# A bf16 feed-forward layer on one core: the first 512 tokens by three DMA transposes instead of five

## The chip, the cores and the metric

The kernel runs on one NeuronCore of a Trainium2 chip. The metric is the device time of one execution in microseconds (us). Six executions of the kernel before took 126.07 to 126.8 us, with a median of 126.53 us. One more execution was recorded by the hardware profiler; its views are what this document reads. A core has five engines that run side by side, each with its own instruction queue: TensorE (PE, matmuls), VectorE (DVE), ScalarE (ACT), GpSimd (POOL) and SyncE (SP, which here issues nearly all DMAs). Sixteen DMA engines move the data.

## The reference

```python
B, S, D, F = 1, 2048, 640, 1728        # x: [B,S,D], w1: [D,F], w2: [F,D], all bf16
h = jnp.einsum("bsd,df->bsf", x, w1)
h = silu(h)
out = jnp.einsum("bsf,fd->bsd", h, w2)
```

## The kernel before

TensorE contracts over the 128 partitions of its two operands. The contraction of the first matmul runs over D = 640, which is five tiles of 128 (`DT` is 5; the code counts them by `k` or `dt`). Both operands must therefore have D on the partitions. w1 has that already. x does not, so it is transposed on its way in: `turned` (L119) issues a DMA transpose on SP's queue which reads 512 tokens by 128 columns of x from DRAM and writes 128 partitions by 512 tokens of `xT` in SBUF. The 2048 tokens are four chunks of 512 (`SCH`), so x takes 4 x 5 = 20 such transposes.

The hidden dimension F = 1728 is 13 tiles of 128 and a tail of 64. The first layer writes hidden units on the partitions: for a chunk and a hidden tile `ft`, five matmuls of 128x128 by 128x512 add up in one PSUM bank, and ACT applies silu and writes `hT`. The second layer then contracts over `hT` with `w2s`; its results leave through `o_sb`. The second layer is not touched by the change.

The first chunk is done differently from the others, because its data has not all come yet. The loop over `k` is outside: `k_pass(k)` (L183) runs hidden tiles 0 to 7, one bank each, with contraction tile `k` alone. All eight banks are thus filled in five passes of eight matmuls. Pass `k` needs transpose `k` of the first chunk and slab `k` of w1 (rows `k` x 128 and on, the first 1024 columns, 256 KB). It waits for both (L193), which is the only thing that TensorE waits for in this stretch. The first slab comes in two halves, so that four matmuls of pass 0 need half a slab only. After the five passes, hidden tiles 8 to 12 of the first chunk follow, from two further loads of w1 (`FG`, tiles 8 to 10 and the rest). Then come chunks 1 to 3 with `k` inside, each after a wait for its transposes, and then the tail and the second layer.

The order of the issues is written out by hand, and a queue issues in that order:

- ACT issues the first half of slab 0 at the very start.
- SP issues transpose 0, the second half of slab 0, transpose 1, slab 1, transpose 2, slab 2, transpose 3, slab 3, transpose 4, slab 4, then the two `FG` loads, the 15 transposes of chunks 1 to 3, and the loads of w2.

What `ahead_of_start` wraps is moved in front of the start barrier of the program. On SP this holds for everything up to slab 1; the drain of the barrier stands behind it (L354 in the profile is where the program is built), and the rest follows. `barrier_wait_here` moves an engine's wait for the others to a later place: behind the `FG` loads on SP, behind pass 0 on PE.

`dummies(15)` (L172) are matmuls on a tile of zeros that nobody reads. They keep TensorE at work until the first data is there. They write bank 3, which pass 0 then overwrites.

Of the kernel before, what the change touches and what calls it, by code (L numbers as in the profile page):

```python
# [9 lines left out]
def bass_standalone__dense_activation_silu__prompt_kernel(  # L10
# [9 lines left out]
    xf = x.flatten_outer_dims()  # L20
# [3 lines left out]
    P = 128  # L24
    NB = 8
    BANK = 512
    DT = D // P
    FT = F // P
    FL = F - FT * P
    SCH = 512  # L30
# [7 lines left out]
    pe, act, dve, pool, sp = nc.tensor, nc.scalar, nc.vector, nc.gpsimd, nc.sync  # L38

    with ExitStack() as es:  # L40
        def sb(name, shape, dtype):
            return es.enter_context(nc.sbuf_tensor(name, shape, dtype))

        xT = sb("xT", [P, DT, S], bf16)
        w1s = sb("w1s", [P, DT, F], bf16)
# [13 lines left out]
        def sem(name):  # L59
            s = es.enter_context(nc.semaphore(name))  # L60
            count[s.name if hasattr(s, "name") else name] = 0
            return [s, 0]

        def tick(ins, s, n=1):
            ins.then_inc(s[0], n)
            s[1] += n
            return (s, s[1])

        def wait(eng, *points):
            for pt in points:  # L70
                if pt is None:
                    continue
                s, v = pt
                key = (id(eng), id(s))
                if seen.get(key, 0) < v:
                    eng.wait_ge(s[0], v)
                    seen[key] = v
# [6 lines left out]
        def load(eng, out_ap, in_ap):  # L84
            s = sem(f"s_ld{n_dma[0]}")
            n_dma[0] += 1
            return tick(eng.dma_start(out=out_ap, in_=in_ap), s, 16)  # L87

        ET = mybir.EngineType

        def preamble(engine, opcode):
            lst = nc.main_func.blocks[0].instructions
            return next(
                i for i, ins in enumerate(lst)
                if ins.opcode == opcode and ins.engine == engine
            )

        def ahead_of_start(emit, engine):
            lst = nc.main_func.blocks[0].instructions
            n = len(lst)  # L100
            r = emit()
            lst = nc.main_func.blocks[0].instructions
            new = lst[n:]
            del lst[n:]
            at = preamble(engine, "Drain")
            lst[at:at] = new
            return r
# [5 lines left out]
        w1_v = w1.rearrange("(dt p) f -> p dt f", p=P)  # L113
        w2_v = w2[0:F0, :].rearrange("(ft p) d -> p ft d", p=P)

        FA = 8
        FG = [(8, 11), (11, FT)]

        def turned(c, dt, s):  # L119
            return tick(sp.dma_start_transpose(  # L120
                out=xT[:, dt, c * SCH:(c + 1) * SCH],
                in_=xf[c * SCH:(c + 1) * SCH, dt * P:(dt + 1) * P],
            ), s, 16)

        def load_k(eng, k):
            return load(eng, w1s[:, k, 0:FA * P], w1_v[:, k, 0:FA * P])

        ld_w1 = {}
        s_x = [sem(f"s_x{k}") for k in range(DT)]
        p_z = ahead_of_start(lambda: tick(dve.memset(z[:, :], 0.0), s_dve), ET.DVE)  # L130
        ld_x = [ahead_of_start(lambda: turned(0, 0, s_x[0]), ET.SP)]
        FH = FA // 2
        ld_k0a = ahead_of_start(
            lambda: load(act, w1s[:, 0, 0:FH * P], w1_v[:, 0, 0:FH * P]), ET.Activation)
        ld_k = [ahead_of_start(
            lambda: load(sp, w1s[:, 0, FH * P:FA * P], w1_v[:, 0, FH * P:FA * P]), ET.SP)]
        ld_x.append(ahead_of_start(lambda: turned(0, 1, s_x[1]), ET.SP))
        ld_k.append(ahead_of_start(lambda: load_k(sp, 1), ET.SP))
        for k in range(2, DT):
            ld_x.append(turned(0, k, s_x[k]))  # L140
            ld_k.append(load_k(sp, k))
        for a, b in FG:
            e = F if b == FT else b * P
            pt = load(sp, w1s[:, :, a * P:e], w1_v[:, :, a * P:e])
# [8 lines left out]
        ld_xc = {}  # L153
        for c in range(1, NSC):
            s = sem(f"s_xc{c}")
            for dt in range(DT):
                ld_xc[c] = turned(c, dt, s)
        ld_w2 = [
            load(sp, w2s[:, 0:7, :], w2_v[:, 0:7, :]),
            load(sp, w2s[:, 7:FT, :], w2_v[:, 7:FT, :]),  # L160
# [6 lines left out]
        def dummies(n):  # L167
            for _ in range(n):
                pe.matmul(ps[:, 3, 0:HB], lhsT=z[:, 0:P], rhs=z[:, :], start=True, stop=True)  # L169

        wait(pe, p_z)
        dummies(15)  # L172

        def mm(o, l, r, start, stop, shared=False):
            return pe.matmul(o, lhsT=l, rhs=r, start=start, stop=stop, skip_group_check=shared)  # L175
# [7 lines left out]
        def k_pass(k):  # L183
            for ft in range(FA):
                if k == 0 and ft == FH:
                    wait(pe, ld_k[0])
# [35 lines left out]
        for q in range(NSC // 2):  # L222
            b = bank()
            for k in range(DT):
                for hh in range(2):
                    c = 2 * q + hh
# [92 lines left out]
        for q in range(NSC // 2):  # L319
            tt = []  # L320
            for hh in range(2):
                c = 2 * q + hh
# [3 lines left out]
            for hh in range(2):  # L326
                c = 2 * q + hh
# [3 lines left out]
                    out=o_sb[:, c * JB:(c + 1) * JB, DA:D],  # L331
                    in_=oT[:, c * SCH:(c + 1) * SCH],
# [36 lines left out]
```

## Time and profile before

| | |
|---|---|
| median of six runs | 126.53 us (126.07 to 126.8) |
| the profiled execution's own time | 126.29 us |
| its span, first to last instruction | 125.0 us |
| PE busy | 121.8 us, 97% of the span |
| ACT busy / DVE busy | 38.1 us / 7.5 us |
| DMA transposes of x | 20, issued at L120 on SP |
| matmuls in the dummies (L169) | 15, 3.38 us |
| first matmul of pass 0 / pass 1 / last pass | 3.57 / 6.44 / 12.42 us after the span's start |

A page of the profile has one line per group of instructions with the line of the code, the engine, the operation and the tiles it writes and reads. A "q" behind an engine (SPq) stands for its queue issuing a DMA, with the time that the issue holds the queue; that time is not the time of the transfer. The view by DMA gives the time from an issue's start to the landing of its data. "Idle before" is what an engine stood still, with the event that ended it. The chain that ended last follows the execution back from its last instruction, at each step to what released it.

### The profile page before, as it was taken

The page shows a single profiled execution, that of the slowest core. Times are in us where ns is not written, and L with a number is a line of the kernel's source. Part 1 is how long each engine was busy: PE and PEld are TensorE (multiplying, and loading weights), DVE is VectorE, ACT ScalarE, POOL GpSimd, SP SyncE. Part 2 cuts the span into 40 slices and gives each one's busy share as a digit, 9 for nine tenths or more (in the row PEclk, how much of TensorE's full clock was granted, in tenths as well). Part 3 has the DMA queues.
Part 4 walks back from the last instruction along what each step waited for, and adds up shares of the span by engine and source line. Part 5 has one row for each costly group of instructions (what it writes and reads, how often), then busy time and mean ns, then how long its engine had stood idle before and what let it go on. Part 6 is the DMA issues. An engine that isn't in the chain of part 4 may idle for free.

```text
span 125.0 us, 1354 instructions
## 1 busy us (share of the span) xinstructions
PE 121.8 (97%) x589; PEld 55.3 (44%) x589; DVE 7.5 (6%) x12; ACT 38.1 (30%) x66; POOL 0.3 (0%) x5
## 2 busy tenths in 40 slices
PE   8998999999999999999999999999999999999993
PEld 6342444444444444444434444444434443444452
DVE  0000000000000000000002020200012210112021
ACT  0400885555555555555530101010012011010100
POOL 0000000000000000000000000000000000000000
DMA  5789957454895000000000000000002868111112
GB/s 109 183 214 229 285 121 77 91 110 93 172 394 210 0 5 0 3 0 0 0 0 0 5 0 0 0 0 0 0 0 64 67 213 302 52 52 52 52 59 99
DMA packets 19541, 10.35 MB, mean 83 GB/s; under 512 B 13520, under 2 KB 19024, under 8 KB 19536
## 3 DMA queue, kind: packets, MB, share of 16 engines
q1 hardware_dynamic: 19392, 10.15, 32.2%
q10 hardware_dynamic: 144, 0.13, 0.4%
q8 instruction: 4, 0.07, 0.2%
q14 instruction: 1, 0.01, 0.0%
HBM read 4.51 MB, written 2.62 MB: 57 GB/s over the span
## 4 chain that ended last, share of the span: by engine, by line
PE 89%; SPq 7%; DMA 3%; issue 1%; ACT 0%
PE ps L175 89%; SPq L120 5%; DMA w1s<-in_w_dram 3%; SPq L87 2%; ACT o_sb L241 0%; SPq L354 0%
## 5 line engine op out<-in xcount | busy, mean ns | idle before, releaser
L175 PE MATMUL ps<-xT,w1s 128*128 128x512 bf16 (+1 forms) x280 | 59.6, 382 | 0.9 <-DMA w1s<-in_w_dram 0.7
L175 PE MATMUL ps<-w2s,hT 128*128 128x512 bf16 (+2 forms) x221 | 45.4, 367 | 0.0
L175 PEld LDWEIGHTS ps<-xT,w1s 128*128 128x128 bf16 (+1 forms) x280 | 26.4, 99 | 33.9 <-issue 3.4
L179 ACT ACTIVATE hT<-ps 128x512 bf16<-128x512 f32 x52 | 30.0, 608 | 26.8 <-PE ps L175 26.8
L175 PEld LDWEIGHTS ps<-w2s,hT 128*128 128x128 bf16 x221 | 20.9, 98 | 24.4 <-issue 1.1
L241 ACT CAST o_sb<-ps 128x512 bf16<-128x512 f32 (+1 forms) x8 | 4.4, 545 | 42.2 <-PE ps L175 42.2
L239 DVE CAST o_sb<-ps 128x512 bf16<-128x512 f32 (+1 forms) x9 | 6.1, 677 | 101.5 <-PE ps L175 101.5
L175 PE MATMUL ps<-hT,w2s 128*128 128x512 bf16 x52 | 11.4, 379 | 0.0
L175 PEld LDWEIGHTS ps<-hT,w2s 128*128 128x128 bf16 x52 | 5.1, 97 | 6.2
L241 ACT CAST oT<-ps 128x512 bf16<-128x512 f32 x2 | 1.1, 588 | 11.0 <-PE ps L175 11.0
L169 PE MATMUL ps<-z 128*128 128x256 bf16 x15 | 3.4, 416 | 0.4 <-DVE z L130 0.4
L169 PEld LDWEIGHTS ps<-z 128*128 128x128 bf16 x15 | 2.0, 142 | 1.2 <-DVE z L130 0.4
L151 ACT ACT_TABLE_LOAD x1 | 1.3, 1283 | 4.1 <-DVEq L354 4.1
L175 PE MATMUL ps<-w2t,hTt 64*128 64x512 bf16 (+2 forms) x17 | 2.2, 366 | 0.0
L239 DVE CAST oT<-ps 128x512 bf16<-128x512 f32 x2 | 1.3, 687 | 13.7 <-PE ps L175 13.7
L179 ACT ACTIVATE hTt<-ps 128x512 bf16<-128x512 f32 x2 | 1.2, 597 | 1.1 <-PE ps L175 1.1
L175 PEld LDWEIGHTS ps<-w2t,hTt 64*128 64x128 bf16 x17 | 0.7, 94 | 1.4 <-issue 0.8
L175 PE MATMUL ps<-hTt,w2t 64*128 64x512 bf16 x4 | 0.6, 381 | 0.0
L175 PEld LDWEIGHTS ps<-hTt,w2t 64*128 64x128 bf16 x4 | 0.1, 94 | 0.4 <-issue 0.4
L151 ACT ACTIVATE warm<-warm 128x32 f32<-128x32 f32 x1 | 0.2, 229 | 0.0
L130 DVE MEMSET z<- 128x128 uint32 x1 | 0.2, 165 | 0.2 <-issue 0.2
L149 POOL MEMSET warm<- 128x32 f32 x1 | 0.1, 124 | 3.7 <-POOLq L354 3.7
(4 smaller groups left out, 0.4 us busy)
## 6 DMA issues: line engine op xcount, KB each, us to landing
out_dram<-o_sb SPq DMA_DIRECT2D x15, 160.0 KB, 1.9
w2s<-in_w_dram SPq DMA_DIRECT2D x1, 1120.0 KB, 5.6
w1s<-in_w_dram SPq DMA_DIRECT2D x4, 256.0 KB, 3.2
w2s<-in_w_dram SPq DMA_DIRECT2D x1, 960.0 KB, 7.6
w1s<-in_w_dram SPq DMA_DIRECT2D x1, 480.0 KB, 4.3
w1s<-in_w_dram SPq DMA_DIRECT2D x1, 400.0 KB, 5.3
xT<-in_x_dram SPq DMA_TRANSPOSE x20, 3.6
w2t<-in_w_dram SPq DMA_DIRECT2D x2, 80.0 KB, 7.0
```

What stands on the lines that cost most here:

```text
L87: return tick(eng.dma_start(out=out_ap, in_=in_ap), s, 16)
L120: return tick(sp.dma_start_transpose(out=xT[:, dt, c * SCH:(c + 1) * SCH], in_=xf[c * SCH:(c + 1) * SCH, dt * P:(dt + 1) * P],), s, 16)
L130: p_z = ahead_of_start(lambda: tick(dve.memset(z[:, :], 0.0), s_dve), ET.DVE)
L149: p_warm = tick(pool.memset(warm[:, :], 0.0), s_pool)
L151: act.activation(out=warm[:, :], in_=warm[:, :], func=ACT.Silu)
L169: pe.matmul(ps[:, 3, 0:HB], lhsT=z[:, 0:P], rhs=z[:, :], start=True, stop=True)
L175: return pe.matmul(o, lhsT=l, rhs=r, start=start, stop=stop, skip_group_check=shared)
L179: r = tick(act.activation(out=out_ap, in_=in_ap, func=ACT.Silu), s_act)
L239: r = tick(dve.tensor_copy(out=out_ap, in_=in_ap), s_dve)
L241: r = tick(act.copy(out=out_ap, in_=in_ap), s_act)
```

## The change

The first chunk's five transposes become three. Their column ranges are `KT` = (0,1), (1,3), (3,5) in contraction tiles: one transpose of 512 x 128 and two of 512 x 256. A wide one writes two rows of `xT`'s middle dimension, and each of its two passes waits for the same semaphore. The same three pieces are used in chunks 1 to 3, so x takes 12 transposes instead of 20. SP's order becomes: transpose 0, second half of slab 0, slab 1, transpose of tiles 1 and 2 (all this ahead of the start barrier), slab 2, transpose of tiles 3 and 4, slab 3, slab 4, and then as before. The dummies go from 15 to 13.

```diff
-        def turned(c, dt, s):
+        def turned(c, k0, k1, s):
             return tick(sp.dma_start_transpose(
-                out=xT[:, dt, c * SCH:(c + 1) * SCH],
-                in_=xf[c * SCH:(c + 1) * SCH, dt * P:(dt + 1) * P],
+                out=xT[:, k0:k1, c * SCH:(c + 1) * SCH],
+                in_=xf[c * SCH:(c + 1) * SCH, k0 * P:k1 * P],
             ), s, 16)
...
-        s_x = [sem(f"s_x{k}") for k in range(DT)]
+        KT = [(0, 1), (1, 3), (3, DT)]
+        s_x = [sem(f"s_x{k0}") for k0, _ in KT]
+        ld_x = {}
+
+        def first(i):
+            k0, k1 = KT[i]
+            pt = turned(0, k0, k1, s_x[i])
+            for k in range(k0, k1):
+                ld_x[k] = pt
...
-        ld_x = [ahead_of_start(lambda: turned(0, 0, s_x[0]), ET.SP)]
...
+        ahead_of_start(lambda: first(0), ET.SP)
...
-        ld_k = [ahead_of_start(
-            lambda: load(sp, w1s[:, 0, FH * P:FA * P], w1_v[:, 0, FH * P:FA * P]), ET.SP)]
-        ld_x.append(ahead_of_start(lambda: turned(0, 1, s_x[1]), ET.SP))
-        ld_k.append(ahead_of_start(lambda: load_k(sp, 1), ET.SP))
-        for k in range(2, DT):
-            ld_x.append(turned(0, k, s_x[k]))
-            ld_k.append(load_k(sp, k))
+        ld_k[0] = ahead_of_start(
+            lambda: load(sp, w1s[:, 0, FH * P:FA * P], w1_v[:, 0, FH * P:FA * P]), ET.SP)
+        ahead_of_start(lambda: slab(1), ET.SP)
+        ahead_of_start(lambda: first(1), ET.SP)
+        slab(2)
+        first(2)
+        slab(3)
+        slab(4)
...
-            for dt in range(DT):
-                ld_xc[c] = turned(c, dt, s)
+            for k0, k1 in KT:
+                ld_xc[c] = turned(c, k0, k1, s)
...
-        dummies(15)
+        dummies(13)
```

More of the change, by code (lines that the diff above doesn't have):

```diff
@@ L128, in bass_standalone__dense_activation_silu__prompt_kernel, with slab @@
         ld_w1 = {}
-        s_x = [sem(f"s_x{k}") for k in range(DT)]
+        KT = [(0, 1), (1, 3), (3, DT)]
[6 more added lines that the diff above has]
+                ld_x[k] = pt
         p_z = ahead_of_start(lambda: tick(dve.memset(z[:, :], 0.0), s_dve), ET.DVE)
-        ld_x = [ahead_of_start(lambda: turned(0, 0, s_x[0]), ET.SP)]
         FH = FA // 2
+        ld_k = {}
+        def slab(k):
+            ld_k[k] = load_k(sp, k)
+        ahead_of_start(lambda: first(0), ET.SP)
         ld_k0a = ahead_of_start(
             lambda: load(act, w1s[:, 0, 0:FH * P], w1_v[:, 0, 0:FH * P]), ET.Activation)
-        ld_k = [ahead_of_start(
-            lambda: load(sp, w1s[:, 0, FH * P:FA * P], w1_v[:, 0, FH * P:FA * P]), ET.SP)]
-        ld_x.append(ahead_of_start(lambda: turned(0, 1, s_x[1]), ET.SP))
-        ld_k.append(ahead_of_start(lambda: load_k(sp, 1), ET.SP))
-        for k in range(2, DT):
-            ld_x.append(turned(0, k, s_x[k]))
-            ld_k.append(load_k(sp, k))
+        ld_k[0] = ahead_of_start(
[6 more added lines that the diff above has]
+        slab(4)
         for a, b in FG:
```

## The prediction

> **What bounds the kernel now.** I read the page first. TensorE is busy for 97% of the span, and the only thing in its group that it waits for is a w1 load (last columns: idle before, and what ended most of it).
>
> ```profile
> PE 121.8 (97%) x589; PEld 55.3 (44%) x589; DVE 7.5 (6%) x12; ACT 38.1 (30%) x66; POOL 0.3 (0%) x5
> ...
> L175 PE MATMUL ps<-xT,w1s 128*128 128x512 bf16 (+1 forms) x280 | 59.6, 382 | 0.9 <-DMA w1s<-in_w_dram 0.7
> ```
>
> The chain that ended last, in order of time, says where the rest is: up to 12.28 us it runs on SP's queue and one w1 transfer, after that on TensorE alone.
>
> ```profile
> 0.00 1.25 SPq L120
> 1.25 0.06 issue
> 1.30 0.56 SPq L87
> ...
> 3.74 0.12 SPq L354
> 3.87 0.07 issue
> 3.93 1.12 SPq L120
> 5.05 0.04 issue
> 5.10 0.58 SPq L87
> ...
> 8.68 3.61 DMA w1s<-in_w_dram
> 12.28 0.14 issue
> 12.42 110.61 PE ps L175 x541
> ```
>
> The reader is to see two things. The 541 matmuls from 12.42 us on hardly pause (110.61 / 541 = 0.204 us each), so the change can win or lose only by moving 12.42, the start of pass 4. And what sets 12.42 is SP: a transpose holds its queue for 1.12 us, a slab for 0.58 us, with gaps the pair takes 1.79 us (3.93 to 5.72), so slab 4 is issued at 8.68 and lands 3.61 us later. The timeline of TensorE shows the same from its side:
>
> ```profile
> 3.57 2.49 PE L175 MATMUL ps<-xT,w1s 128*128 128x512 bf16 x8
> 6.44 5.63 PE L175 MATMUL ps<-xT,w1s 128*128 128x512 bf16 x24 [0.38 <-DMA w1s<-in_w_dram]
> 12.42 0.81 PE L175 MATMUL ps<-xT,w1s 128*128 128x512 bf16 x3 [0.35 <-DMA w1s<-in_w_dram]
> ```
>
> The single starts in the trace are: pass 1 at 6.44, pass 2 at 8.16, pass 3 at 10.18, pass 4 at 12.42; a pass of eight takes 1.73 us. Passes 1, 3 and 4 start 0.135 us after their slab's last semaphore count (6.31, 10.05, 12.28). Against four passes in a row from 6.44, 12.42 - 6.44 - 3 x 1.73 = 0.79 us is lost; and 0.5 us more lies between the end of pass 0 (5.9) and 6.44. So some 1.3 us, 1%, is all there is to win.
>
> The DMA engines in the same stretch, in windows (last two columns: busy share, GB/s):
>
> ```profile
> 4.30:6.30 2.00, 1.76 (x7) 0.54 (x5) 0.00 (x0) 1.30 (x2) 0.00 (x0) 1.00 0.85 194
> 6.30:8.10 1.80, 1.66 (x8) 0.71 (x8) 0.00 (x0) 0.00 (x0) 0.00 (x0) 1.00 0.92 222
> 8.10:9.90 1.80, 1.80 (x10) 0.73 (x8) 0.00 (x0) 0.00 (x0) 0.00 (x0) 1.00 0.91 214
> ```
>
> They are 85 to 92% busy: freeing SP soon meets them.
>
> **The change part by part.** The unknown is how long SP is held by a transpose of 512 x 256; call it X. Every transpose in the trace has the same size (128 KB), so X is bounded: below by the row itself, 1.12 us, if an issue costs the same whatever it moves; above by twice that, 2.24 us.
>
> SP's new order, from the rows above: transpose 0 to 1.25; second half of slab 0, 1.30 to 1.87; slab 1, 1.92 to 2.50 (before: 3.11); wide transpose A from 2.54 to 2.54 + X; the barrier's drain and gaps, 0.25; slab 2 from 2.79 + X to 3.37 + X; wide transpose B from 3.41 + X to 3.41 + 2X; slab 3 to 4.03 + 2X; slab 4 from 4.07 + 2X. With X = 1.12 slab 4 is issued at 6.31, with 2.24 at 8.55, against 8.68. Slab 3 goes out at 3.45 + 2X, against 6.89: later than before as soon as X is over 1.72.
>
> Which X? In the trace's packet records a plain load's first packet comes 0.55 to 0.6 us after its issue ends; a transpose of the quiet stretch from 14 us on sends its first 0.11 us after its issue of 1.26 us ends. So the work on the data seems handed over some 0.45 us before the issue ends, and the part that could grow with the size is 0.7 to 0.8 us of it, not all. A plain load with 640 pieces per transfer holds SP for 0.43 us and one with 128 pieces for 0.58 us: the issue of a load does not grow with its pieces. **I take X = 1.45**, nearer the row than its double, with 1.12 and 2.24 kept for the range.
>
> [...]
>
> The **transfers** follow SP in one queue. From the packet records: a slab's packets start 0.6 us after its issue ends and take 1.06 us of all engines' busy time (128 packets of 2 KB per 16 engines, 132 ns each), some 1.3 us from first to last; a transpose's 512 packets take 0.57 us busy, 0.75 to 0.85 from first to last; the last semaphore count comes about 0.5 us after the last packet. I take 1.2 us for a slab and 1.3 us for a wide transpose, between busy time and spread. After the change with X = 1.45:
> - Slab 1: packets 3.1 to 4.5, landed at about 5.1 (before: 6.31).
> - A: issue ends at 3.99, packets behind slab 1, 4.5 to 5.8, landed at 6.3. Pass 1 starts at 6.4. **What is late next:** the releaser of pass 1 becomes the transpose instead of the slab, at about the same time. Nothing won here.
> - Slab 2: issued to 4.82, packets 5.8 to 7.0, landed at 7.5; pass 2 at 6.4 + 1.73 = 8.15 finds it there.
> - B: issued to 6.31, packets 7.0 to 8.3, landed at 8.8. Slab 3: issued to 6.93, packets 8.3 to 9.5, landed at 10.0 against its turn at 9.9. Pass 3 starts between 9.9 and 10.15.
> - Slab 4: packets to 10.7, landed at 11.2. Its pass follows pass 3 without a wait: 9.9 + 1.73 = 11.63 to 11.9, against 12.42.
>
> So pass 4 comes 0.5 to 0.8 us earlier; I take 0.63. Up to X of about 1.7 the engines, not SP, set this; the point where nothing is won is pass 3 at 10.69, slab 3's packets ending at 10.05, B's starting at 7.55, so 3.41 + 2X + 0.35 = 7.55 and X = 1.9.
>
> **The dummies.** Two fewer take away 2 x 0.213 us (their spacing), so pass 0 starts at 3.14; transpose 0 lands at 2.8 and the first half of slab 0 at 2.26, both in time. Its fifth matmul wants the other half, landed at 4.19, before four matmuls of 0.43 us are over (4.8). Pass 0 ends at 5.7 instead of 5.9, in front of the wait for A: worth nothing, up to 0.2 us if A is early. The cover they gave is not needed as long as A lands after 5.6.
>
> **The rest of the queue.** The `FG` loads move up with slab 4 (issued from 7.6 instead of 9.30; the first landed at 13.61, wanted at 14.14 before and 13.5 now; after slab 4's packets at 10.7 its 480 KB need 2.2 us as before, so 13.3: hidden with little to spare). Chunks 1 to 3 have nine issues of 1.26 + 2X instead of 15 of 1.26: SP is free earlier unless X doubles, where it is equal. Chunk 1 landed at 18.58 and was wanted at 19.54; an issue moved up by 1 us or more keeps that. w2 is wanted at 64 us and landed at 39.8. All at nothing; without cover, a late chunk 1 would cost its lateness above the slack of 0.96 us.
>
> **The sum:** SP 0 by itself, pass 4 by -0.63, the others 0: the profiled span 125.0 becomes 124.4, its execution 126.29 becomes 125.66. The profiled one is 0.24 under the median of the runs shown; from the median, 126.53 - 0.63 = **125.9 us**.
>
> **The rivals.**
> - *The wide issue costs its double* (ends slower). X = 2.24: A's issue ends at 4.78, its packets 5.1 to 6.4, pass 1 at 7.05. B's issue ends at 7.89, packets 8.25 to 9.5, slab 3 to 10.7, landed at 11.2, pass 3 at 11.35, pass 4 at 13.1: 0.65 us later, 127.2 us. It decides from X = 1.9. [...] Against it: the packets that start right behind the issue.
> - *The DMA engines are the bound anyway* (no change). If slab and wide transpose keep their full spreads, 1.3 and 1.6 us, then from 4.5 us A ends at 6.1, slab 2 at 7.4, B at 9.0, slab 3 at 10.3, pass 3 at 10.9: 126.5 to 126.7 us. For it: 0.9 busy. Against it: in the window from 12.3 to 14.1 us the same engines moved 352 GB/s, against 214 here, so part of that busy time is waiting.
> - *More overlap than I allow*: busy times alone put A's last packet at 5.35 and pass 1 at 6.0; then all passes follow, pass 4 at 11.2, 1.2 us earlier: 125.3 us.
>
> **How the numbers follow.** The forecast (X under 1.7, 125.5 to 126.2) has 0.48, more overlap 0.12, the DMA bound 0.16, the double issue 0.24. A measurement of this kernel can tell about 0.3%, 0.38 us. The two first are faster, less 0.03 for the forecast's weak end: 0.57. Same: 0.16 + 0.03 and a little of the double issue with X near 1.9, 0.2. Slower: 0.23. The range runs from the overlap case to the double issue, 125.3 to 127.2; the likeliest alone, 125.5 to 126.2.
>
> **What would show it.** SP's rows at L120 for the first chunk with the wide issue's duration (1.45 right, over 1.9 wrong); slab 4's issue near 7 us; pass 1 released by the transpose near 6.4; pass 3 with a wait under 0.3 us; pass 4 near 11.7; the long run of matmuls unchanged at 110.6 us. The prediction is wrong if the wide issue is near 2.2 us, or if the DMA share rises to 1 with slab 3 still landing after 10.5.

## The result and the profile after

The changed kernel takes 125.83 us (median of 27 runs, 125.43 to 126.31) against 126.39 us (median of 62) for the kernel before: a ratio of 0.9948, 95% interval 0.9935 to 0.9962. That is 0.5% faster; forecast was 125.9 us. Ratios, here and below, leave out the few slow runs, those over 1.5% above the fastest of their kernel; medians count every run.

The page of the changed kernel, busy time of the engines and the matmul group that holds the first layer:

```profile
PE 121.2 (98%) x587; PEld 55.1 (44%) x587; DVE 7.5 (6%) x12; ACT 38.1 (31%) x66; POOL 0.3 (0%) x5
...
L189 PE MATMUL ps<-xT,w1s 128*128 128x512 bf16 (+1 forms) x280 | 59.5, 382 | 0.7 <-DMA xT<-in_x_dram 0.6
```

TensorE's waits are now put down to a transpose of x; before, it was a slab of w1. The chain that ended last, in order of time, says where the gain is:

```profile
0.00 1.24 SPq L120
1.24 0.06 issue
1.29 0.57 SPq L87
1.86 0.05 issue
1.92 0.42 SPq L87
2.33 0.04 issue
2.38 3.89 DMA xT<-in_x_dram
6.26 0.05 issue
6.31 3.63 PE ps L189 x16
9.94 0.07 issue
10.01 112.34 PE ps L189 x549
```

SP leaves this chain at 2.38 us; before, it was in it until 8.68. From 6.31 us on TensorE runs, with one short stop ahead of pass 3, which is at 10.01. The 549 matmuls from there are pass 3 and the rest, so pass 4 starts 1.73 us later, at 11.73 in the records of single matmuls, against 12.42 before. That is 0.69 us, and the spans differ by as much (125.0 and 124.3). Nothing behind pass 4 has moved.

The other traces say the same more sharply. In all fourteen of this case, the two kernels and the twelve edits below, the recorded execution's own time is the start of its pass 4 plus 113.86 or 113.87 us. So a time tells where pass 4 began. By this sum the medians, 126.39 and 125.83 us, stand for pass 4 at an estimated 12.52 and 11.96 us: the two traces, with 12.42 and 11.73, are of executions somewhat faster than the usual one.

SP's part of the timeline shows why it left (start, time held):

```profile
2.38 1.26 SPq L120 DMA_TRANSPOSE xT<-in_x_dram  x1
4.14 0.33 SPq L87 DMA_DIRECT2D w1s<-in_w_dram  x1
4.52 1.24 SPq L120 DMA_TRANSPOSE xT<-in_x_dram  x1
5.80 2.10 SPq L87 DMA_DIRECT2D w1s<-in_w_dram  x4
```

A transpose of 512 x 256 holds SP for 1.24 to 1.26 us, one of 512 x 128 held it for 1.12 to 1.25. In this stretch the second half of the columns is all but free to issue.

### The profile page after: what moved, and what is told of

It reads as the page before. It is cut to its first block, busy times and chain, and to the rows that moved or that the text cites. A ratio compares the mean times of both kernels' runs of the same rounds, so it can differ in the third digit from the quotient of the medians.

```text
span 124.3 us, 1340 instructions
## 1 busy us (share of the span) xinstructions
PE 121.2 (98%) x587; PEld 55.1 (44%) x587; DVE 7.5 (6%) x12; ACT 38.1 (31%) x66; POOL 0.3 (0%) x5
## 3 DMA queue, kind: packets, MB, share of 16 engines
q1 hardware_dynamic: 19136, 10.15, 32.3%
## 4 chain that ended last, share of the span: by engine, by line
PE 93%; DMA 3%; SPq 2%; issue 0%; ACT 0%
PE ps L189 93%; DMA xT<-in_x_dram 3%; SPq L120 1%; SPq L87 1%; ACT o_sb L255 0%
```

## The experiments

All are edits of the changed kernel. Each was timed in five rounds beside the kernel before on the same chip. Theory M, from the prediction: the gain is the merging, since a wide issue costs SP no more; what then sets the passes is the transfers. Its rivals: O, the gain is the order (slab 1 ahead of the transpose); D, it is the dummies.

**The order without the merging.** Each wide transpose is taken apart into two in a row.

```diff
-        KT = [(0, 1), (1, 3), (3, DT)]
+        KT = [(k, k + 1) for k in range(DT)]
...
         ahead_of_start(lambda: first(1), ET.SP)
+        ahead_of_start(lambda: first(2), ET.SP)
         slab(2)
-        first(2)
+        first(3)
+        first(4)
```

> The changed kernel's order of issues and its 13 dummies, with each wide transpose taken apart into two single ones in a row (also in chunks 1 to 3). Theory M (the gain is the merging: a wide issue holds SP no longer than a single one): two more issues of 1.12 to 1.26 us put slab 3's issue near 8.05 instead of 5.80, its landing near 11.25, pass 3 at 11.4, pass 4 at 13.1 against 12.42 in the kernel before: ratio to the kernel before about 1.005. Theory O (the order of the issues gives the gain): ratio 0.995, pass 4 near 11.7.

Measured: 127.35 us, ratio 1.0051 (1.0029 to 1.0073). Its chain, in order of time, has SP in it all the way to slab 3:

```profile
2.39 1.15 SPq L120
3.54 0.04 issue
3.58 1.26 SPq L120
...
5.71 1.13 SPq L120
6.85 0.04 issue
6.89 1.25 SPq L120
8.14 0.04 issue
8.19 3.11 DMA w1s<-in_w_dram
11.29 0.14 issue
11.43 112.34 PE ps L191 x549
```

Slab 3 is issued at 8.19 instead of 5.80 and pass 3 starts at 11.43 instead of 10.01. The later issue is two more transposes of some 1.2 us each and nothing else. The order alone makes the kernel slower than before; O as the sole cause falls. (Slab 1 moved ahead by itself, with the single transposes left one by one between the slabs, was not tried.)

**The merging without the order.** Each wide transpose goes ahead of its slab.

```diff
-        ahead_of_start(lambda: slab(1), ET.SP)
         ahead_of_start(lambda: first(1), ET.SP)
-        slab(2)
+        ahead_of_start(lambda: slab(1), ET.SP)
         first(2)
+        slab(2)
```

> Wide transposes, each ahead of the slab as in the kernel before (transpose 0, half slab, A, slab 1, B, slab 2, slab 3, slab 4), 13 dummies. Theory M: the bytes in front of pass 3 are the same, so pass 3 near 10.0 to 10.2 and pass 4 near 11.7 to 11.9; pass 1 is released by slab 1 near 6.5; ratio 0.994 to 0.997. Theory O: without slab 1 ahead the gain is gone, ratio 0.999 or more.

Measured: 127.82 us, ratio 1.0075 (1.0048 to 1.0103). This is a miss for M, which had called the order indifferent. First the chain, then TensorE's timeline of this kernel:

```profile
4.05 1.23 SPq L120
5.28 0.04 issue
5.33 5.63 DMA w1s<-in_w_dram
10.95 0.05 issue
11.00 114.08 PE ps L189 x557
```

```profile
7.20 1.89 PE L189 MATMUL ps<-xT,w1s 128*128 128x512 bf16 x8 [1.53 <-DMA w1s<-in_w_dram]
11.00 4.27 PE L189 MATMUL ps<-xT,w1s 128*128 128x512 bf16 x19 [1.92 <-DMA w1s<-in_w_dram]
```

The recorded execution took 128.33 us, the longest of this kernel's runs (127.34 to 128.33), so its delays are larger than the usual ones. SP is as early as wanted (slab 2 issued at 5.33), but the slabs that followed a wide transpose landed late. Slab 1 lands at 7.06 and pass 1 starts at 7.20; in the changed kernel the same two transfers, the other way round, are both there at 6.26. In the packet records, wide transpose and slab together take 3.2 us from the start of the first packet to that of the last here (3.40 to 6.61), and 2.6 us in the changed kernel (3.07 to 5.68). Then slab 2 takes 5.6 us to land. The sixteen semaphore counts that make up its landing come from 8.68 to 10.95: twelve within 0.1 us, the last four over 1.8 us. So the merging needs the order to be a gain: each is worth over 1% in the presence of the other (1.0051 and 1.0075 against 0.9948).

**The dummies.** `dummies(15)` instead of 13.

> The changed kernel with 15 dummies again. Theory M: pass 0 ends 0.2 to 0.4 us later, still before the wide transpose lands at 6.26, so nothing changes: ratio 0.994 to 0.996. Theory D (the two dummies are part of the gain): 0.4 us back, ratio 0.998.

Measured: 125.93 us, ratio 0.9926 (0.9898 to 0.9955): no part of the gain that can be told is theirs, as the prediction had it. D falls.

**The later chunks.** Chunks 1 to 3 by single transposes.

```diff
-            for k0, k1 in KT:
-                ld_xc[c] = turned(c, k0, k1, s)
+            for k in range(DT):
+                ld_xc[c] = turned(c, k, k + 1, s)
```

> The changed kernel with chunks 1 to 3 by single transposes (15 issues) as in the kernel before. Theory M: SP has more than the slack it needs there, chunk 1 is wanted near 19; nothing changes: ratio 0.994 to 0.996. If the merging in the later chunks were a part of the gain: ratio 0.997 or more.

Measured: 126.01 us, ratio 0.9955 (0.9938 to 0.9971). The merging there is worth nothing that can be told.

**Wider still.** The first chunk by one transpose of one tile and one of four, the later chunks by single ones.

```diff
-        KT = [(0, 1), (1, 3), (3, DT)]
+        KT = [(0, 1), (1, DT)]
...
         slab(2)
-        first(2)
         slab(3)
```

> First chunk by two transposes, one of one tile and one of four (512 KB); slabs 2 to 4 behind it; chunks 1 to 3 by single ones. If an issue costs the same whatever it moves: the one of four holds SP 1.1 to 1.4 us. If it grows by tiles: 0.5 us or more over the one of two, so 1.8 us or more. Its 2048 packets, 512 KB at the rate of the wide ones (256 KB in 1.2 to 1.5 us), need 2.5 to 3 us from about 4.1 on, so it lands near 7.4, pass 1 starts near 7.5, and the others follow every 1.73 us: pass 4 near 12.7, ratio about 1.002.

Measured: 126.22 us, ratio 0.9957 (0.9936 to 0.9977). SP's timeline and the chain of this kernel:

```profile
2.39 3.00 SPq L120 DMA_TRANSPOSE xT<-in_x_dram  x1
5.89 2.33 SPq L87 DMA_DIRECT2D w1s<-in_w_dram  x5
```

```profile
2.39 5.10 DMA xT<-in_x_dram
7.49 0.05 issue
7.54 115.81 PE ps L188 x565
```

The passes went as expected: pass 1 at 7.54 and no stop after it. The ratio did not: 1.002 was expected. The recorded execution, at 126.59 us, is near the top of this kernel's runs (126.03 to 126.68); it does stand at 1.002 to the recorded one of the kernel before (126.29), but the usual run is faster, and no trace shows where. The issue went neither way that was expected: no more for two tiles than for one, then 3.00 us for four. To see whether that was a queue full of earlier transfers, chunk 2 was moved by one transpose of five tiles and chunk 3 by one of one and one of four, late, where SP has nothing pressing:

```diff
-            for k0, k1 in KT:
+            for k0, k1 in {1: KT, 2: [(0, DT)], 3: [(0, 1), (1, DT)]}[c]:
```

> The changed kernel; chunk 2's transposes are one of five tiles, chunk 3's one of one and one of four, both in the quiet stretch where nothing waits for SP. If the 3.0 us of the issue of four in the first stretch were its size: 3 us or more again, 3.7 for five. If they were a queue full of the transfers ahead: near 1.3 to 1.4 us for both, apart from the one issue in this stretch that is 1.0 to 1.3 us longer in every run so far. The time is that of the changed kernel: ratio 0.993 to 0.997.

Measured: 125.79 us, ratio 0.9934 (0.9908 to 0.9960), the changed kernel's time as expected. The issues of five tiles and of four in SP's timeline:

```profile
14.05 3.45 SPq L120 DMA_TRANSPOSE xT<-in_x_dram  x1
18.84 3.75 SPq L120 DMA_TRANSPOSE xT<-in_x_dram  x1
```

Within the second lies an instruction fetch (16 KB, on its own queue, at 19.06). The issue of four began with 262 earlier packets still to start in the first stretch and with 551 here, and was long both times. So for it the size is enough; the five began behind 1,526 and cannot tell. The packet records give a form to it. When SP came free, there were still to go: 1,469 of the 2,048 packets of the four in the first stretch, 1,487 of the 2,560 of the five, 1,542 of the 2,048 of the four here. In these three rows SP was held until some 1,500 packets were left to start. Two tiles are 1,024 packets and do not reach this by themselves.

But a queue full of earlier transfers does it too. In the changed kernel's own trace the first two transposes of chunk 1, of one tile and of two, come right behind the `FG` loads:

```profile
8.03 1.67 SPq L120 DMA_TRANSPOSE xT<-in_x_dram  x1
9.73 2.33 SPq L120 DMA_TRANSPOSE xT<-in_x_dram  x1
```

They began with 1,510 and 1,755 packets issued before them and not yet started, and SP came free with 1,772 and 1,685; no instruction fetch lies beside them. In the second experiment the one tile at this place held SP for 3.39 us. So what holds SP looks like the number of packets outstanding on the queue, whoever's they are. No single limit fits every row: in the kernel before, the second transpose of chunk 1 took 1.26 us with 1,671 packets ahead of it. Three tiles (1,536 packets) were not tried.

**Are the bytes the bound up to pass 3?** Slabs 1 to 4 bring half their columns in the first stretch; passes 1 to 4 use columns 0 to 511 for hidden tiles 4 to 7 too, so this kernel leaves the other columns out of the first chunk's result. They come later, for chunks 1 to 3.

```diff
-            return load(eng, w1s[:, k, 0:FA * P], w1_v[:, k, 0:FA * P])
+            return load(eng, w1s[:, k, 0:FH * P], w1_v[:, k, 0:FH * P])
...
+        late = [load(sp, w1s[:, 1:DT, FH * P:FA * P], w1_v[:, 1:DT, FH * P:FA * P])]
         barrier_wait_here(ET.SP)
...
+                fw = ft % FH if k else ft
-                ins = mm(ps[:, ft, :], w1s[:, k, ft * P:(ft + 1) * P], xT[:, k, 0:SCH],
+                ins = mm(ps[:, ft, :], w1s[:, k, fw * P:(fw + 1) * P], xT[:, k, 0:SCH],
```

> The changed kernel with half the bytes of slabs 1 to 4 in the first stretch (columns 0 to 511; the other columns come behind the FG loads in one load, and chunks 1 to 3 wait for it). Passes 1 to 4 use columns 0 to 511 for hidden tiles 4 to 7 too, so the first chunk's result is not the reference's there. The issues on SP keep their number. If the DMA engines bound the changed kernel up to pass 3: A's packets start near 4.1 and need no longer wait for slab 1's, A lands near 5.6, pass 1 at 5.7, the others follow without a wait, pass 4 at 10.9, ratio 0.988 to 0.990. If SP or a fixed time of landing bounds it: pass 1 stays near 6.3, pass 4 near 11.5 to 11.7, ratio 0.993 to 0.995.

Measured: 125.29 us, ratio 0.9901 (0.9871 to 0.9931). The chain:

```profile
5.80 3.86 DMA w1s<-in_w_dram
9.66 0.14 issue
9.79 112.34 PE ps L191 x549
```

Pass 1 came at 5.92 instead of 6.31. That the bytes ahead of it count there is not shown: the fourth experiment's trace, with whole slabs, has it at 6.02. Slab 3, with half its bytes and 256 KB less in front of it, still landed 3.86 us after its issue at 5.80, at 9.66. With whole slabs and the same first stretch on SP it landed at 9.87 in the changed kernel's trace, at 9.96, 10.28 and 10.07 in those of `dummies(15)`, of the single later chunks and of the wider later chunks. So the slabs' bytes are at most a small part of what makes pass 3 wait. A rival is left: this edit halves neither the number of a slab's packets (128) nor the two wide transposes in front.

**What is behind a slab.** In the traces so far a slab with a transpose behind it mostly had its sixteen counts close together (slab 2 in the changed kernel: 6.87 to 6.95), one with plain loads behind it had them spread (slab 3: 8.91 to 9.87). (The half slab 1 of the last experiment, 3.97 to 4.76 with A behind it, is an exception.) Theory S, a guess: engines that finish a slab early go on with the next load and take from those still at work on the slab. Chunk 1's transpose of one tile was put behind slab 3.

```diff
         slab(3)
+        turned(1, 0, 1, s_xc[1])
         slab(4)
```

> The changed kernel with chunk 1's transpose of one tile issued between slab 3 and slab 4. The bytes ahead of slab 3 are the same. Theory S (a slab with further plain loads behind it lands late because the engines that finish early go on with the next load while the slow ones still have pieces; a transpose behind it holds the fast ones): slab 3's sixteen counts come within 0.3 us instead of 0.96 us, the last near 9.0 instead of 9.87, pass 3 follows pass 2 at 9.77, pass 4 near 11.5 if slab 4 (0.6 us more in front of it) lands by 11.4; ratio 0.992 to 0.994. Theory B (the bytes in front of it set slab 3's landing): 9.8 to 10.0 again, pass 4 at 11.7 or later, ratio 0.995 or more.

Measured: 125.92 us, ratio 0.9953 (0.9930 to 0.9976). All but the first of slab 3's counts came together, from 9.84 to 9.98, but no earlier than before: the spread closed from its early end. In this execution slab 2 and B had landed 0.9 us later than in the changed kernel's trace (B at 8.91); the kernel with the wider later chunks, whose first stretch is the changed kernel's, had the same delay (B at 8.96) and slab 3 at 10.07. So 0.1 us at most can be put down to the edit. This is what theory B expected, down to the ratio. The wait moved on to slab 4, which has plain loads behind it; fifteen of its counts were there by 11.22, the last came at 12.54:

```profile
7.59 4.95 DMA w1s<-in_w_dram
12.54 0.05 issue
12.58 1.04 PE ps L192 x4
```

The same edit behind slab 2 in the kernel of the second experiment:

> The kernel with wide transposes ahead of their slabs (slab 2's sixteen counts there came from 8.68 to 10.95, with slabs 3 and 4 right behind it), with chunk 1's transpose of one tile issued between slab 2 and slab 3. Theory S: slab 2's counts end near 8.8 to 9.0, pass 2 at 9.0 instead of 11.0, pass 4 near 12.5, ratio 0.999 to 1.002. Theory B: slab 2 as late as before, slabs 3 and 4 later still, ratio 1.007 or more.

Measured: 127.22 us, ratio 1.0058 (1.0040 to 1.0077). Slab 2's counts were 9.26 to 9.44 instead of 8.68 to 10.95, so pass 2 came 1.5 us earlier; then slab 3, which now had slab 4 behind it, had the spread (10.52 to 11.79), and pass 3 waited for that. Here both theories missed: S by 1.1 us in pass 4 (13.65, about 12.5 expected), B by calling slab 2 as late as before. A transpose behind a slab did hold its counts together, in both runs (9.84 to 9.98 but for the first, and 9.26 to 9.44); it brought the last one forward in one run and not in the other. What makes slab 3 of the changed kernel land near 9.9 is left open; the next experiment has one more hint.

**Trying to win more.** Slab 3 in two halves with a semaphore each, so that pass 3 can start on the first:

```diff
         def slab(k):
-            ld_k[k] = load_k(sp, k)
+            if k == 3:
+                ld_k[k] = load(sp, w1s[:, k, 0:FH * P], w1_v[:, k, 0:FH * P])
+                ld_3b.append(load(sp, w1s[:, k, FH * P:FA * P], w1_v[:, k, FH * P:FA * P]))
+            else:
+                ld_k[k] = load_k(sp, k)
...
+                if k == 3 and ft == FH:
+                    wait(pe, *ld_3b)
```

> The changed kernel with slab 3 loaded in two halves, each with its own semaphore, so that the first four matmuls of pass 3 need half a slab. Theory M with the DMA engines as the next bound: pass 3 loses its wait of 0.23 us, pass 4 starts 0.1 to 0.2 us earlier, ratio 0.993 to 0.994. If the extra issue on SP (0.45 to 0.58 us) delays slab 4 (needed at 11.5, landed at 10.5): still hidden.

Measured: 125.35 us, ratio 0.9915 (0.9885 to 0.9945). The chain:

```profile
2.37 3.88 DMA xT<-in_x_dram
6.26 0.05 issue
6.30 115.81 PE ps L194 x565
```

The stop ahead of pass 3 is gone: 565 matmuls in a row from pass 1 on, and pass 4 at 11.49. The halves landed at 8.95 and 9.46, so the whole of slab 3 was there 0.4 us earlier than in the changed kernel's trace, with the same bytes and one issue more. One trace shows this, and no run tells why. Of the kernels that leave nothing out it has the lowest median here, and it beats the kernel before clearly; its lead over the changed kernel (0.3%) is inside the intervals.

Slab 1 from ACT's queue:

```diff
-        ahead_of_start(lambda: slab(1), ET.SP)
+        ld_k[1] = ahead_of_start(lambda: load_k(act, 1), ET.Activation)
```

> The changed kernel with slab 1 issued by ACT, behind its half of slab 0, so that A goes out on SP 0.47 us earlier (1.91). If the DMA engines bound pass 1: slab 1 now runs beside transpose 0 and the second half of slab 0, those land up to 1 us later, A lands 0.3 to 0.5 us earlier, pass 1 near 5.9, pass 3 still near 9.7 to 10.0 by its slab: ratio 0.992 to 0.995. If pass 0 is held up by the late half slab: pass 1 unchanged, ratio 0.995 to 0.998.

Measured: 126.98 us, ratio 0.9969 (0.9936 to 1.0002). The median is of 22 executions; the ratio keeps 13 of them and says little, since they fall into two groups. Slab 1 now ran beside transpose 0, which landed at 4.33 instead of 3.04, more than the 1 us that was allowed for, and pass 0 started at 4.38. What came of it is under the last heading.

Four pieces, the first two of one tile:

```diff
-        KT = [(0, 1), (1, 3), (3, DT)]
+        KT = [(0, 1), (1, 2), (2, 4), (4, DT)]
...
         slab(3)
+        first(3)
         slab(4)
```

> First chunk by four transposes (tiles 0; 1; 2 and 3; 4), in the order transpose 0, half slab 0, slab 1, tile 1, slab 2, tiles 2 and 3, slab 3, tile 4, slab 4; the same pieces in the later chunks. Each of slabs 1 to 3 has a transpose behind it, and pass 1 needs 128 KB less in front of it. If issues cost by number and the landings follow theory S: tile 1 lands near 5.4, pass 1 at 5.5, pass 2 near 7.7 (waits for tiles 2 and 3), pass 3 at 9.5, pass 4 at 11.2: ratio 0.990 to 0.992, under the changed kernel by 0.4 us. If the one more issue of SP (1.12 us) comes back as a late slab 4 (issued near 7.5, landed near 11.0 or later): pass 4 at 11.7 or more, ratio 0.995.

Measured: 125.90 us, ratio 0.9938 (0.9911 to 0.9964), not to be told from the changed kernel. Tile 1 landed at 5.79, 0.47 us before the wide A, but the additional issue came back as the second expectation said: slab 4 went out at 7.50 instead of 6.42, landed at 12.05, and pass 4 started at 12.19 in the recorded execution (126.05 us, near the top of its runs).

## Why the prediction was right

- **What bounds it, and how much there is to win.** Right: SP's issues up to slab 4 set pass 4 (two more of them, in the first experiment, moved it by 1.42 us), and the gain is pass 4's move alone, in every trace.
- **X.** Taken as 1.45, measured 1.24 to 1.26, between the ends, 1.12 and 2.24, and near the row. The double is not what a transpose of two tiles costs here: twice the tiles took at most 0.14 us more (1.26 against 1.12). The row decided, and it holds for two tiles while the queue is not full; at four the issue is 3.00 us. A slab behind another load, taken as 0.58 us, held SP for 0.42 to 0.43, which helped too: slab 3 went out at 5.80, not 6.35 (3.45 + 2 x 1.45). The rival of the double issue (127.2 us) falls.
- **The landings.** Slab 1: forecast 5.1, measured 5.15. A: 6.3, 6.26. Pass 1: 6.4, 6.31. Slab 2: 7.5, 6.95. B: 8.8, 7.98. Slab 3: 10.0, 9.87. Pass 3: 9.9 to 10.15, 10.01. Slab 4: 11.2, 10.52. Pass 4: 11.63 to 11.9, 11.73; the gain forecast as 0.63 us is 0.69 in the trace and 0.56 between the medians. Part of this closeness is the draw: in the three other traces with the same first stretch on SP pass 4 came at 11.82, 11.93 and 12.14. That the releaser of pass 1 becomes the transpose was right too.
- **Why slab 3 is there near 10.** Here the reason was wrong where the number was right. The step took the DMA engines to work through the bytes in order, each slab 1.2 us and each wide transpose 1.3. B was there 0.8 us before its forecast, so by this step slab 3 should have landed near 9.2; it landed at 9.87, and with half the bytes still at 9.66. The errors cancelled, and that is luck. In the four traces with this first stretch B landed at 7.98, 8.12, 8.19 and 8.96, and slab 3 at 9.87, 9.96, 10.28 and 10.07: it does not follow B. The landing is the last of sixteen counts, up to 1.5 us behind the first of them, and a sum of bytes over all engines does not see that. What does set it stays open.
- **The order.** The prediction costed moving slab 1 ahead as "nothing won here", because A takes its place as the releaser. That holds for the time of pass 1 against the kernel before. It missed that with A ahead of slab 1 the pair lands at 7.06 instead of 6.26, and that slab 2 then stalls: without this move the merging loses 0.75%.
- **Dummies, `FG` loads, later chunks.** Worth nothing, as forecast: 15 dummies and single later chunks both give the changed kernel's time. The first `FG` load landed at 11.86, wanted at 13.46. Chunk 1 landed at 15.99 instead of 18.58.
- **The rivals left.** That the engines leave no gain (126.5 to 126.7 us) was off by 0.7 us or more, that they overlap to 125.3 us by 0.5 us. The DMA share did rise, as the windows after show against 0.85 to 0.92 before (last two columns: busy share, GB/s):

```profile
4.30:6.30 2.00, 1.38 (x6) 0.39 (x4) 0.00 (x0) 1.51 (x2) 0.12 (x1) 1.00 1.16 270
6.30:8.10 1.80, 1.79 (x9) 0.84 (x10) 0.00 (x0) 0.00 (x0) 0.00 (x0) 1.00 1.16 195
8.10:9.90 1.80, 1.80 (x9) 0.63 (x7) 0.00 (x0) 0.00 (x0) 0.00 (x0) 1.00 0.89 299
```

A share over 1 beside 195 GB/s, with 299 GB/s at 0.89 in the next window, agrees with the prediction that packets' busy time has waiting in it; it is no measure of how much more the engines could move.

## What to carry to other kernels

Where a queue's issues set the start of a matmul-bound kernel, as here, count the issues and not the bytes: a transpose of twice the width cost SP the same 1.25 us as long as the queue had room. With some 1,500 packets outstanding, its own or earlier ones, issues took up to 3.71 us, though one of 512 x 128 with 1,671 ahead of it took 1.26. But merging made the pieces land later and in fewer steps (tile 1 at 6.26 us within A, at 5.79 as a piece of its own), so the order has to be set again with it; here the merging without the new order lost 0.75%, the new order without the merging 0.5%, and both together won 0.5%. Pass 3 started at 10.01, behind the last of slab 3's sixteen counts (8.91 to 9.87), so look at the spread of the counts before summing bytes.

## What the runs showed of the hardware that was not expected

**The issue of a transpose has a step, not a slope.** In a queue with room it held SP for 1.12 to 1.26 us with one tile, 1.23 to 1.30 with two and 3.00 with four, and behind 1,526 earlier packets 3.45 with five; in the three widest issues SP came free with 1,469 to 1,542 packets to go. Behind the `FG` loads one tile took up to 3.39 us and two up to 3.71. Apart from these, each trace has one issue of chunks 2 or 3 that is 0.5 to 1.4 us longer than its like, and in each a 16 KB instruction fetch runs beside it (in the kernel before 2.38 us instead of 1.26, from 19.66, with the fetch at 19.61; in the changed one 2.64 instead of 1.26, from 17.45, with the fetch at 18.21). That the fetch is the cause is read from this coincidence alone.

**TensorE's matmuls doubled their pace at very different times.** Matmuls of 512 columns follow each other every 0.427 us at first and every 0.216 us later. The first fast one came near 4.8 us in the kernel before, 4.4 in the changed one, 3.1 to 6.1 in the others that started alike. With slab 1 on ACT's queue TensorE stood still for 1.03 us ahead of pass 0, and all of pass 0 was slow:

```profile
4.38 9.85 PE L189 MATMUL ps<-xT,w1s 128*128 128x512 bf16 x37 [1.03 <-DMA xT<-in_x_dram]
```

Windows of that kernel over pass 0 and over the same length after it (second column: PE busy and matmuls):

```profile
4.38:7.78 3.40, 3.40 (x9) 1.20 (x10) 0.00 (x0) 0.96 (x2) 0.00 (x0) 1.00 1.09 205
7.78:11.20 3.42, 3.42 (x17) 1.60 (x16) 0.00 (x0) 0.00 (x0) 0.00 (x0) 1.00 0.99 323
```

Nine matmuls against seventeen in the same time, while the column of the granted clock shows 1.00 in both. Its 22 executions fall into two groups, 125.24 to 125.72 us and 126.85 to 127.87 us. The recorded one is in the second group (126.85), and its trace has the slow pass 0, which is 8 x 0.21 = 1.7 us longer than a fast one; that the first group is executions with an early change of pace is argued from this, not recorded, and what makes others of the second group up to 1.0 us longer than the recorded one is not known. Between the earliest and the latest of the traces that started alike lie 3.0 us; what sets the moment no trace shows. In the changed kernel this costs little: a wholly slow pass 0 from 3.14 us would end near 6.55 (3.14 + 8 x 0.427, an estimate), 0.3 us behind A's landing at 6.26; in its trace, with the first fast matmul near 4.4, pass 0 is over at 5.68 and A is waited for.
